# Lightning attention with an ELU layer on one core: a weight slice uncast on SyncE's queue, chunks 0 to 3 in pairs, decayed k made once, and a new order

## The chip, the cores and the metric

One Trainium2 chip, of which the program uses one core. The metric is the device time of one execution in microseconds (us). Three executions of the kernel before took 216.35, 214.18 and 216.23 us, the median is 216.23 us. Lower is better.

## What is computed

Decayed causal attention over `(B, H, S, D) = (4, 8, 768, 64)`, then a two-layer network without a gate:

```python
intra = (q_b @ k_b.T) * Dmask          # Dmask[i, j] = lam**(i - j) for i >= j, else 0
inter = (q_b * lam**(pos + 1)) @ kv_state
attn  = intra @ v_b + inter            # block by block along the sequence
kv_state = lam**block * kv_state + (k_b * lam**(block - 1 - pos)).T @ v_b
x = attn as [3072 tokens, 512]
h = x @ w_in                           # w_in [512, 2048]
g = where(h > 0, h, exp(min(h, 0)) - 1)
out = g @ w_out                        # w_out [2048, 512], out in float32
```

All inputs are float32 in memory. The kernels work in float16 with float32 sums.

## The kernel before

The 3072 tokens are cut into 24 chunks of 128: chunk `g` is sequence block `g // 4` of batch `g % 4`. So chunks 0 to 3 have no state behind them, and chunk `g` needs the state that chunk `g - 4` left. The last four leave none.

**Attention of one chunk.** `T`: q and k are transposed, for chunks 0 to 7 on TensorE (`att_T_pe`, L274: q comes out of PSUM times `qs`, the powers of lambda along the row, on VectorE; k by a copy on ScalarE), for chunks 8 to 23 by DMA transposes on SyncE's queue (`att_T_dma`, L264). `S`: eight matmuls give the scores of the eight heads in two PSUM banks (`att_S`, L294). `E`: VectorE multiplies each half with `mask`, which holds the causal triangle and the other half of the decay (`att_E`, L313). `P`: 8 matmuls with v, and from chunk 4 on 8 more with the state (`att_P`, L327). `X`: the result is written to `xt` in float16, on ScalarE for chunks 0 to 7, on VectorE with `qs` after that. `U`: `kd` (k times its decay, made on GpSimd, `att_kd`, L169) times v gives the state's growth (`att_U`, L388); `M`: GpSimd multiplies the old state with `upp` (`att_M`, L368), and VectorE adds the growth.

**The network.** `mm1` (L467) fills one PSUM tile `psH` of 128 x 512 (two such buffers): for chunks 0 to 3 one chunk by 4 columns of 128 of `w_in`, 16 matmuls of 128 x 128; from chunk 4 on two chunks by 2 columns, 8 matmuls of 128 x 256 (`GSIZE`). ScalarE takes `Exp` and then `Relu` of the tile, VectorE joins them to `g` (`flush`, L452), and this frees the buffer. `mm2` (L490) is 4 matmuls of 128 x 512; four such units make one chunk's output, which ScalarE copies and SyncE's queue stores. The very last columns of chunk 23 come in `mm2_rest` (L506). Each weight is held whole in float16 in 8 slices (`i0` to `i7` of w_in, `o0` to `o7` of w_out, each 256 KB in float16).

**What sets the order.** Every engine works in the order in which the code emits. The opening is written out by hand in `OPEN` (L53); after it a rule (L589 to L628) puts the attention of two chunks ahead of the mm1 units that need them, and up to two mm2 units behind each mm1. GpSimd has an order of its own, `POOL_ORDER` (L47): it issues all casting loads (float32 in memory, float16 on chip), and does `kd` and `M` between them. A load is issued only when the load 8 places ahead of it has landed. Only `lam` and the q of chunk 0 (`raw_q0`, float32, cast on VectorE, L122) come over SyncE's queue. PSUM has the two `psH` buffers and six other banks, given out by `BANKS` and by a rule (L255). Matmuls on zeros keep TensorE busy at the start: 10, then `w2` and `w6` in `OPEN`.

Of the kernel before, what the change touches and what calls it, by code (L numbers as in the profile page):

```python
# [15 lines left out]
def kernel(  # L16
# [26 lines left out]
    GSIZE = {**{g: 1 for g in range(4)}, **{g: 2 for g in range(4, NG, 2)}}  # L43
# [3 lines left out]
    POOL_ORDER = (  # L47
        "k0 k1 iota q1 k2 v1 i0 v0 q2 i1 v2 i2 o0 i3 d0 q3 o1 i4 k3 i5 o2 o3 v3 d1 m4 d2 d3 i7 "
        "o4 o5 i6 o7 k4 o6 q4 m5 k6 v4 q6 k10 q10 d5 d4 d6 m6 v6 k8 q8 v8 d7 m7 v10"
    )  # L50
    RAW = "q0"
    FIRST = "q0:0 c0 c1 c2"
    OPEN = (  # L53
# [7 lines left out]
    )  # L61
    LAGU = 7
    AT = {"L": -18, "W": -13, "T": -9, "S": -8, "B": -4}
    BANKS = (
        "S0=M0,M1 S1=C,D S2=D,M1 S3=D,B P0=M1 P1=B P2=B P3=D U0=M0 U1=D U2=A U3=M1 T0=M1,C "
        "T1=D,A T2=A,D T3=D T4=M0 T5=A T6=M1 T7=D M2=C M3=M0"
# [14 lines left out]
    def zero_matmuls(n):  # L81
# [4 lines left out]
    zero_matmuls(10)  # L86
# [4 lines left out]


# [3 lines left out]
    st = [  # L96
        [cpool.tile([128, NHP, 128], FP16, name=f"st{b}_{i}") for i in range(2)]
        for b in range(B)
    ]
    qg, kg, vg = {}, {}, {}  # L100

    def emit_load(w, g0):
        n = size_of[g0]
        c, b = divmod(g0, B)
        x = {"q": q, "k": k, "v": v}[w]
        src = x[b : b + n, :, c * L : (c + 1) * L].rearrange("b h p d -> p (b h) d")
        t = asb.tile([128, n, H, 64], FP16, tag=f"{w}n{n}", name=f"{w}n{g0}", bufs=4)
# [12 lines left out]
    nc.scalar.preload_act_table_set("natural_log_exp_and_others")  # L120

    def cast_raw(g, w, eng):  # L122
        n = f"{w}{g}"
        t = asb.tile([128, 1, H, 64], FP16, tag=f"{w}n1", name=f"{w}n{g}", bufs=4)
        (qg if w == "q" else kg)[g] = t
        if eng == 0:
            nc.vector.tensor_copy(t[:, 0], raw[n][:])
        else:
            nc.scalar.copy(t[:, 0], raw[n][:])

    def of(tiles, g):
        g0, i = group_of[g]
        return tiles[g0][:, i]
# [18 lines left out]

    def emit_wo(i):
# [9 lines left out]
    def emit_iota():  # L163
        nc.gpsimd.iota(iota_c[:], pattern=[[0, 1]], base=0, channel_multiplier=1)
        nc.gpsimd.iota(iota_r[:], pattern=[[1, 128]], base=0, channel_multiplier=0)

    kds, qkT, Pt, psS, xg = {}, {}, {}, {}, {}

    def att_kd(g):  # L169
        if g // B == NCB - 1:  # L170
            return
        kd = asb.tile([128, H, 64], FP16, tag="kd", name=f"kd{g}", bufs=8)
        kds[g] = kd
        nc.gpsimd.tensor_tensor(  # L174
            out=kd[:], in0=of(kg, g),
            in1=ks[:].unsqueeze(2).broadcast_to([128, H, 64]), op=ALU.mult,
        )


    pool_list = POOL_ORDER.split()  # L180

    def emit_pool():
        w = pool_list.pop(0)
        if w == "iota":
            emit_iota()
        elif w[0] in "qkv":
            emit_load(w[0], int(w[1:]))
        else:
            {"i": emit_wi, "o": emit_wo, "d": att_kd, "m": lambda g: att_M(g)}[w[0]](int(w[1:]))

    def emit_pool_run():
        while pool_list and pool_list[0][0] != "m":
            emit_pool()

    assert "iota" in POOL_ORDER.split("d0")[0]
    while pool_list and pool_list[0][0] not in "dm":
        emit_pool()

    def zero_st1(b):
        nc.vector.memset(st[b][1][:], 0.0)  # L200


    loglam = cpool.tile([128, H], FP32, name="loglam")
    nc.scalar.activation(loglam[:], lam_b[:], AF.Ln)
    pos = cpool.tile([128, 3], FP32, name="pos")
# [4 lines left out]

    dn = cpool.tile([128, H], FP32, name="dn")
    mask = cpool.tile([128, H, 128], FP32, name="mask")
    qs = cpool.tile([128, NHP, 128], FP32, name="qs")
    ks = cpool.tile([128, H], FP32, name="ks")
    upp = cpool.tile([128, NHP], FP32, name="upp")
    nc.vector.tensor_copy(row[:], iota_r[:])
    nc.vector.tensor_copy(pos[:, 0:1], iota_c[:])
    nc.vector.tensor_scalar_mul(pos[:, 1:2], iota_c[:], -1.0)
    nc.scalar.activation(dn[:], loglam[:], AF.Exp, scale=pos[:, 1:2])
    nc.vector.tensor_scalar(  # L220
        out=ident16[:], in0=row[:], scalar1=pos[:, 0:1], scalar2=None, op0=ALU.is_equal
    )
    nc.vector.tensor_scalar(
        out=causT[:], in0=row[:], scalar1=pos[:, 0:1], scalar2=None, op0=ALU.is_ge
    )
    for hh in range(2):
        r = slice(hh * 64, (hh + 1) * 64)
        nc.vector.tensor_copy(loglam_p[r, :], loglam[r, hh::2])
    nc.vector.tensor_scalar_add(pos[:, 2:3], pos[:, 1:2], float(L))

    def emit_qs():
        for hp in range(NHP):
            nc.scalar.activation(
                qs[:, hp, :], row[:], AF.Exp, scale=loglam_p[:, hp : hp + 1]
            )

    def emit_mask():
        nc.vector.tensor_tensor(
            out=mask[:],
            in0=causT[:].unsqueeze(1).broadcast_to([128, H, 128]),  # L240
            in1=dn[:].unsqueeze(2).broadcast_to([128, H, 128]),
            op=ALU.mult,
        )

    def emit_ks():
        nc.scalar.activation(ks[:], loglam[:], AF.Exp, scale=pos[:, 2:3])
        nc.scalar.activation(upp[:], loglam_p[:], AF.Exp, scale=float(L))

# [13 lines left out]


    def att_T_dma(g):  # L264
        ts = []
        for w, tiles in (("q", qg), ("k", kg)):
            t = asb.tile([128, NHP, 128], FP16, tag=f"{w}T", name=f"{w}T{g}", bufs=6)
            nc.sync.dma_start_transpose(
                out=t[:], in_=of(tiles, g).rearrange("p h d -> p (h d)")
            )  # L270
            ts.append(t)
        qkT[g] = ts

    def att_T_pe(g):  # L274
        n = len(TAGS[f"T{g}"].split())
        pts = [
            bank(f"T{g}", i, [128, 2 // n, NHP, 128], FP16, f"psT{g}_{i}")
            for i in range(n)
        ]
        pts = [pts[0][:, 0], pts[n - 1][:, 2 // n - 1]]  # L280
        for src, pt in zip((of(qg, g), of(kg, g)), pts):
            for hp in range(NHP):
                nc.tensor.transpose(  # L283
                    pt[:, hp, :], in_=src[:, 2 * hp : 2 * hp + 2, :], identity=ident16[:]
                )
        qt, kt = [
            asb.tile([128, NHP, 128], FP16, tag=f"{w}T", name=f"{w}T{g}", bufs=6)
            for w in "qk"
        ]
        nc.vector.tensor_tensor(out=qt[:], in0=pts[0], in1=qs[:], op=ALU.mult)  # L290
        nc.scalar.copy(out=kt[:], in_=pts[1])  # L291
        qkT[g] = (qt, kt)

    def att_S(g):  # L294
        qt, kt = qkT[g]
# [11 lines left out]
    late, X_done, Y_done, E_done = [], set(), set(), set()  # L307

    def until(done, g):
        while g not in done:  # L310
            late.pop(0)()

    def att_E(g):  # L313
        pts = psS.pop(g)

        def half(hh):
# [5 lines left out]
            if hh == 1:  # L322
                E_done.add(g)
# [3 lines left out]
    def att_P(g):  # L327
        cb, b = divmod(g, B)
        until(E_done, g)
        if cb > 0:  # L330
            until(Y_done, g - B)
# [295 lines left out]
    for t in prog:  # L627
        run(t)  # L628
# [34 lines left out]
```

## Time and profile before

| | us |
|---|---|
| three executions | 216.35, 214.18, 216.23 |
| span of the profiled execution | 213.2 |
| TensorE busy in it | 202.7 |
| VectorE, ScalarE, GpSimd busy | 130.1, 129.0, 96.2 |
| DMA queue of GpSimd's loads | 13.50 MB |
| DMA queue of SyncE | 10.76 MB |

The span runs from the first to the last instruction that the profiler sees; the time of an execution also holds what lies around it. The time of the profiled execution itself is not listed apart from the three; against their median the span is 3.0 us short. Busy times of TensorE overlap from one matmul to the next, so its pace is read from the starts of consecutive groups.

### The profile page before, as it was taken

The page shows a single profiled execution, that of the slowest core. Times are in us where ns is not written, and L with a number is a line of the kernel's source. Part 1 is how long each engine was busy: PE and PEld are TensorE (multiplying, and loading weights), DVE is VectorE, ACT ScalarE, POOL GpSimd, SP SyncE. Part 2 cuts the span into 40 slices and gives each one's busy share as a digit, 9 for nine tenths or more (in the row PEclk, how much of TensorE's full clock was granted, in tenths as well). Part 3 has the DMA queues.
Part 4 walks back from the last instruction along what each step waited for, and adds up shares of the span by engine and source line. Part 5 has one row for each costly group of instructions (what it writes and reads, how often), then busy time and mean ns, then how long its engine had stood idle before and what let it go on. Part 6 is the DMA issues. An engine that isn't in the chain of part 4 may idle for free.

```text
span 213.2 us, 5156 instructions
## 1 busy us (share of the span) xinstructions
PE 202.7 (95%) x2066; PEld 138.1 (65%) x2066; DVE 130.1 (61%) x224; ACT 129.0 (61%) x245; POOL 96.2 (45%) x115
## 2 busy tenths in 40 slices
PE   7667999999999999999999999999999999999994
PEld 2355676767686776766766766766766666666652
DVE  3936453777846888677667667667667547533321
ACT  4545654884867756676476476476476576477640
POOL 7996991999972908667166259300000000000000
PEclk9999999999999999999999999999999999999999
DMA  8999999999996999999939919999124110110112
GB/s 90 141 175 193 192 148 173 147 165 147 153 165 145 111 197 107 144 122 116 129 106 125 167 59 103 144 180 161 52 65 83 52 49 0 54 51 16 36 49 98
DMA packets 101976, 24.59 MB, mean 115 GB/s; under 512 B 92608, under 2 KB 99008, under 8 KB 101952
## 3 DMA queue, kind: packets, MB, share of 16 engines
q0 software_dynamic: 79760, 13.50, 83.1%
q1 hardware_dynamic: 22192, 10.76, 24.6%
q8 instruction: 16, 0.26, 0.5%
q14 instruction: 8, 0.07, 0.1%
HBM read 27.27 MB, written 6.29 MB: 157 GB/s over the span
## 4 chain that ended last, share of the span: by engine, by line
PE 82%; POOL 8%; DMA 7%; issue 1%; ACT 1%; DVE 0%; POOLq 0%; ACTq 0%
PE psM L499 36%; PE psH L478 35%; DMA wi<-in_moe_w_in_dram 4%; DMA wo<-in_moe_w_out_dram 3%; PE psO L338 3%; PE psS L302 3%; PE psO L344 2%; POOL kd L174 1%; POOL wi L148 1%; POOL kn L109 1%; POOL vn L109 1%; PE psU L406 1%; PE psT L283 1%; POOL qn L109 1%; POOL wo L155 1%
## 5 line engine op out<-in xcount | busy, mean ns | idle before, releaser
L478 PE MATMUL psH<-xt,wi 128*128 128x256 f16 (+1 forms) x896 | 99.3, 258 | 2.0 <-DMA wi<-in_moe_w_in_dram 1.1
L457 DVE SCALAR_TENSOR_TENSOR g<-e,psH 128x512 f16<-128x512 f32 x96 | 65.8, 686 | 56.7 <-ACT psH L485 56.0
L484 ACT ACTIVATE e<-psH 128x512 f32<-128x512 f32 x96 | 57.3, 597 | 65.0 <-PE psH L478 62.8
L499 PE MATMUL psM<-wo,g 128*128 128x512 f16 (+1 forms) x384 | 95.6, 377 | 0.7 <-DMA wo<-in_moe_w_out_dram 0.7
L478 PEld LDWEIGHTS <-wi 128*128 128x128 f16 x896 | 76.9, 98 | 27.4 <-DMA wi<-in_moe_w_in_dram 1.8
L485 ACT ACTIVATE psH<-psH 128x512 f32<-128x512 f32 x96 | 57.0, 593 | 0.0
L499 PEld LDWEIGHTS <-g 128*128 128x128 f16 x384 | 35.9, 98 | 29.3 <-issue 1.3
L318 DVE TENSOR_TENSOR pp<-psS,mask 128x512 f16<-128x512 f32 x48 | 30.8, 684 | 4.4 <-PE psS L302 4.4
L174 POOL TENSOR_TENSOR kd<-kn,ks 128x512 f16<-128x512 f16 x20 | 20.7, 1040 | 21.3 <-DMA kn<-in_k_dram 20.4
L378 POOL TENSOR_TENSOR stt<-st,upp 64x256 f32<-64x256 f16 x32 | 19.5, 608 | 14.7 <-DVE st L418 8.9
L109 POOL DMA_DIRECT2D vn<-in_v_dram x14 | 15.5, 1108 | 1.7 <-DMA wi<-in_moe_w_in_dram 1.7
L109 POOL DMA_DIRECT2D kn<-in_k_dram x14 | 15.5, 1105 | 0.8 <-POOLq L647 0.8
L525 ACT COPY osb<-psM 128x512 f32<-128x512 f32 x23 | 13.5, 590 | 3.2 <-PE psM L499 3.2
L109 POOL DMA_DIRECT2D qn<-in_q_dram x13 | 14.8, 1138 | 0.0
L418 DVE TENSOR_TENSOR st<-stt,psU 64x256 f16<-64x256 f32 x32 | 13.3, 416 | 1.2 <-PE psU L406 0.5
L361 DVE TENSOR_TENSOR xt<-psO,qs 128x512 f16<-128x512 f32 x16 | 11.0, 688 | 3.5 <-PE psO L344 3.5
L338 PE MATMUL psO<-pp,vn 128*64 128x128 f16 x192 | 12.0, 222 | 1.2 <-DMA vn<-in_v_dram 1.0
L338 PEld LDWEIGHTS <-vn 128*64 128x64 f16 x192 | 9.7, 110 | 4.6 <-issue 2.9
L344 PE MATMUL psO<-qT,st 128*64 128x128 f16 x160 | 10.0, 219 | 0.0
L344 PEld LDWEIGHTS <-st 128*64 128x64 f16 x160 | 8.9, 110 | 0.0
L302 PE MATMUL psS<-qT,kT 64*128 64x128 f16 x192 | 7.9, 218 | 0.3 <-ACT kT L291 0.3
L359 ACT CAST xt<-psO 128x512 f16<-128x512 f32 x8 | 4.4, 588 | 6.4 <-PE psO L338 4.3
(44 smaller groups left out, 72.3 us busy)
## 6 DMA issues: line engine op xcount, KB each, us to landing
out_dram<-osb SPq DMA_DIRECT2D x23, 256.0 KB, 2.2
kn<-in_k_dram POOLq DMA_DIRECT2D x10, 256.0 KB, 7.8
qn<-in_q_dram POOLq DMA_DIRECT2D x10, 256.0 KB, 6.8
vn<-in_v_dram POOLq DMA_DIRECT2D x10, 256.0 KB, 7.6
wi<-in_moe_w_in_dram POOLq DMA_DIRECT2D x8, 256.0 KB, 6.9
wo<-in_moe_w_out_dram POOLq DMA_DIRECT2D x8, 256.0 KB, 7.7
kn<-in_k_dram POOLq DMA_DIRECT2D x4, 128.0 KB, 4.2
vn<-in_v_dram POOLq DMA_DIRECT2D x4, 128.0 KB, 5.5
```

The source lines that it names most:

```text
L109: nc.gpsimd.dma_start(out=t[:].rearrange("p b h d -> p (b h) d"), in_=src)
L174: nc.gpsimd.tensor_tensor(out=kd[:], in0=of(kg, g), in1=ks[:].unsqueeze(2).broadcast_to([128, H, 64]), op=ALU.mult,)
L302: nc.tensor.matmul(psS[g][hh][:, hp, :], lhsT=kt[r, hp, :], rhs=qt[r, hp, :], start=True, stop=True,)
L318: nc.vector.tensor_tensor(out=P[:], in0=pts[hh][:], in1=mask[:, hh::2, :], op=ALU.mult)
L338: nc.tensor.matmul(po[r, hp, :], lhsT=vt[:, 2 * hp + hh, :], rhs=Pt[(g, hh)][:, hp, :], start=True, stop=(cb == 0), skip_group_check=True,)
L344: nc.tensor.matmul(po[r, hp, :], lhsT=st[b][cb % 2][:, hp, r], rhs=qt[:, hp, :], start=False, stop=True, skip_group_check=True,)
L378: nc.gpsimd.tensor_tensor(out=tmp[r], in0=old[r, :, r], in1=upp[r].unsqueeze(2).broadcast_to([64, NHP, 64]), op=ALU.mult,)
L457: nc.vector.scalar_tensor_tensor(out=g[:].rearrange("p f c t -> p (f c t)"), in0=e[:], scalar=-1.0, in1=r[:], op0=ALU.add, op1=ALU.min,)
L478: nc.tensor.matmul(pH[:, f * n * 128 : (f + 1) * n * 128], lhsT=wi16[i][:, kk, w * 128 : (w + 1) * 128], rhs=xg[g0][:, kk, :], start=(kk = ...
L484: nc.scalar.activation(e[:], pH[:], AF.Exp)
L485: nc.scalar.activation(pH[:], pH[:], AF.Relu)
L499: nc.tensor.matmul(psM[g][:, cols], lhsT=gts[(g, j * FB + f)], rhs=wo16[i][:, w, cols], start=first and f == 0, stop=end and f == FB - 1, ...
```

## The change

- **Opening loads.** `raw_q0` goes; slice `i1` of w_in comes in float32 over SyncE's queue (512 KB), and ScalarE casts it (`cast_wi`). q of chunk 0 becomes a casting load of GpSimd. GpSimd's order becomes `k0 q0 k1 i3 (iota) q1 k3 q3 v0 v1 q2 k2 i2 v2 i0 v3 k4 q4 o2 o3 v4 (kd5) i4 o1 o0 i7 k6 i6 q6 o7 i5 o6 o4 o5 (kd7 kd6) k8 ...`. Before, it was `k0 k1 (iota) q1 k2 v1 i0 v0 q2 i1 v2 i2 o0 i3 (kd0) q3 o1 i4 k3 i5 o2 o3 v3 (kd1, M4, kd2, kd3) i7 o4 o5 i6 o7 k4 o6 q4 ...`.
- **Pairs.** `GSIZE` is 2 everywhere: mm1 has 96 units of 8 matmuls of 128 x 256 (before 16 units of 16 matmuls of 128 x 128, and 80 of 8).
- **Decay of k.** `kd` is made for all 24 chunks, 11 of them on VectorE (0 to 3 and 4, 10, 14, 15, 20, 22, 23), and it is `kd`, not k, that is transposed; so `E` multiplies with the plain triangle `causT`, and `mask` and `dn` go.
- **State.** VectorE adds the growth to the state in float32, and GpSimd multiplies the sum with `upp` into the state (before: GpSimd first, VectorE last); for the first block VectorE does the product alone.
- **Order.** One list `ORDER` holds every step of every engine. The zero matmuls are the first 10 alone. Banks are in `BANKS` for every step. The last units are `R` (`mm2_rest`), then mm2 of chunks 22 and 19.

The diff, cut to its core:

```diff
-    GSIZE = {**{g: 1 for g in range(4)}, **{g: 2 for g in range(4, NG, 2)}}
+    GSIZE = {g: 2 for g in range(0, NG, 2)}
-    RAW = "q0"
-    FIRST = "q0:0 c0 c1 c2"
+    RAW = "i1S"
+    ORDER = (
+        "z:0:1:v z:1:1:v L:k0 z:1:0:a L:q0 L:k1 log logp i:3 upp c:1:a iota col L:q1 row ks caus qs:0 qs:2 "
+        "ident qs:1 d:0:v qs:3 L:k3 t:q0 z:0:0:v t:k0 e:q0:v L:q3 e:k0:a d:1:v s:0 L:v0 t:k1 E:0:0 e:k1:a "
+        "E:0:1 L:v1 t:q1 e:q1:v L:q2 d:3:v s:1 L:k2 E:1:0 t:q3 t:k3 e:q3:v e:k3:a i:2 u:0 p:0 E:1:1 s:3 x:0:a "
+        "L:v2 E:3:0 p:1 z:2:0:a x:1:a y:0 i:0 t:q2 z:2:1:a 1:0:3 E:3:1 L:v3 d:2:v 1:0:1 h:0:3 e:q2:v L:k4 "
+        "t:k2 e:k2:a g:0:3 L:q4 h:0:1 s:2 1:0:2 E:2:0 o:2 E:2:1 h:0:2 o:3 g:0:1 p:2 u:2 x:2:v L:v4 u:3 p:3 "
+        "u:1 g:0:2 1:0:0 x:3:a z:3:1:v 1:2:0 h:0:0 d:5:p d:4:v y:1 t:k4 i:4 h:2:0 t:k5 g:0:0 t:q4 o:1 t:q5 "
+        "e:q4:v 1:2:1 e:k4:a o:0 g:2:0 s:4 h:2:1 e:q5:v i:7 1:2:2 E:4:0 L:k6 2:1:1 e:k5:a E:4:1 h:2:2 g:2:1 "
+        "s:5 i:6 2:0:1 E:5:1 L:q6 y:3 1:2:3 g:2:2 o:7 u:4 h:2:3 p:4 E:5:0 u:5 i:5 1:2:4 y:5 x:4:a g:2:3 p:5 "
...
+        "g:22:4 2:20:0 h:20:6 2:22:2 g:20:6 2:23:2 2:20:3 2:21:3 R 2:22:0 2:19:2"
+    )
+    def cast_wi(i, eng):
+        if eng == "a":
+            nc.scalar.copy(out=wi16[i][:], in_=raw[f"i{i}"][:])
...
+    def att_kd(g, eng="p"):
+        kd = asb.tile([128, H, 64], FP16, tag="kd", name=f"kd{g}", bufs=8)
+        kds[g] = kd
+        {"v": nc.vector, "p": nc.gpsimd}[eng].tensor_tensor(
+            out=kd[:], in0=of("k", g),
+            in1=ks[:].unsqueeze(2).broadcast_to([128, H, 64]), op=ALU.mult,
+        )
...
+    def att_E(g, hh):
+        P = asb.tile([128, NHP, 128], FP16, tag="pp", name=f"pp{g}_{hh}", bufs=6)
+        nc.vector.tensor_tensor(
+            out=P[:], in0=psS[g][hh][:],
+            in1=causT[:].unsqueeze(1).broadcast_to([128, NHP, 128]), op=ALU.mult,
+        )
...
+    def att_Y(g, hh):
...
+            nc.vector.tensor_tensor(
+                out=tmp[r], in0=stp[b][cb % 2][r, :, r], in1=src, op=ALU.add
+            )
```

In `ORDER`, `L`, `i` and `o` are loads; `d` is `kd`; `t` and `e` are a TensorE transpose and its way out of PSUM; `D` a DMA transpose; `s`, `E`, `p`, `x`, `u` are the steps named above; `y` and `m` the state on VectorE and on GpSimd; `1:g:j` a unit of mm1, `h` its two ScalarE steps, `g:` VectorE's join; `2:g:j` a unit of mm2. A last letter `a`, `v` or `p` says ScalarE, VectorE or GpSimd. So `1:2:4` is the unit of chunks 2 and 3 on slice `i4`.

More of the change, by code (lines that the diff above doesn't have):

```diff
@@ L161 @@
     iota_r = cpool.tile([128, 128], I32, name="iota_r")
[L163 to L200, printed above, removed]
     loglam = cpool.tile([128, H], FP32, name="loglam")
-    nc.scalar.activation(loglam[:], lam_b[:], AF.Ln)
-    pos = cpool.tile([128, 3], FP32, name="pos")
+    col = cpool.tile([128, 2], FP32, name="col")
     row = cpool.tile([128, 128], FP32, name="row")
@@ L219 @@
[L219 to L242, printed above, removed]
-        )
-    def emit_ks():
-        nc.scalar.activation(ks[:], loglam[:], AF.Exp, scale=pos[:, 2:3])
-        nc.scalar.activation(upp[:], loglam_p[:], AF.Exp, scale=float(L))
+    def emit_iota():
+        nc.gpsimd.iota(iota_c[:], pattern=[[0, 1]], base=-L, channel_multiplier=1)
+        nc.gpsimd.iota(iota_r[:], pattern=[[1, 128]], base=-L, channel_multiplier=0)
@@ L397, in att_U @@
+    def att_U(g):
+        if g < B:
+            pu = bank(f"U{g}", 0, [128, NHP, 64], FP32, f"psU{g}")
+        elif g % 2 == 0:
+            psUU[g] = bank(f"U{g}", 0, [128, 2, NHP, 64], FP32, f"psU{g}")
+            pu = psUU[g][:, 0]
+        else:
+            pu = psUU[g - 1][:, 1]
+        vt = of("v", g)
+        for hp in range(NHP):
+            for hh in range(2):
+                r = slice(hh * 64, (hh + 1) * 64)
                 nc.tensor.matmul(
-                    full[:, hp, :].rearrange("p (h e) -> p h e", h=2),
@@ L445 @@
-    gts, psM, stores, pending = {}, {}, [], []
+                    pu[r, hp, :], lhsT=kds[g][:, 2 * hp + hh, :], rhs=vt[:, 2 * hp + hh, :],
+                    start=True, stop=True, skip_group_check=True,
+                )
+        psU[g] = pu
+    gts, psM, psH, stores, pending = {}, {}, {}, [], {}
     def emit_stores(keep=0):
@@ L627 @@
-    for t in prog:
-        run(t)
-    mm2_rest()
-    while late:
-        late.pop(0)()
+    CONST = {
+        "iota": emit_iota, "col": const_col, "row": const_row, "log": const_log,
+        "qn": const_qn, "ks": const_ks, "ident": const_ident, "caus": const_caus,
+        "logp": const_logp, "upp": const_upp,
+    }
+    def run(t):
+        if t in CONST:
+            CONST[t]()
+            return
+        w, *a = t.split(":")
+        n = [int(x) if x.isdigit() else x for x in a]
+        if w in "Late" and a[0][0] in "qkv":
+            x, g = a[0][0], int(a[0][1:])
+            {"L": emit_load, "a": scaled, "t": att_T_pe, "e": att_T_out}[w](x, g, *a[1:])
+        elif w == "D":
+            att_T_dma(a[0][0], int(a[0][1:]))
+        elif w == "y":
+            att_Y(n[0], 0)
+            att_Y(n[0], 1)
+        else:
+            {"qs": const_qs, "z": zero_st, "w": zero_matmuls, "i": emit_wi, "o": emit_wo,
+             "c": cast_wi, "d": att_kd, "s": att_S, "E": att_E, "p": att_P, "x": att_X, "u": att_U,
+             "m": att_M, "1": mm1, "h": elu_in, "R": mm2_rest, "g": elu_out, "2": mm2}[w](*n)
@@ L632 @@
+    for t in ORDER.split():
+        run(t)
     emit_stores()
```

404 lines of the change are left out of this document (138 added, 266 removed), and 50 rows, old and new, of tables (BANKS, OPEN, ORDER).

## Prediction

> **What bounds the kernel now.** I read the page first (shares, slices, chain), then windows of 10 us, then TensorE's timeline, and at last the DMA view on windows so narrow that they hold one load, which gives its landing.
>
> ```profile
> span 213.2 us, 5156 instructions
> PE 202.7 (95%) x2066; PEld 138.1 (65%) x2066; DVE 130.1 (61%) x224; ACT 129.0 (61%) x245; POOL 96.2 (45%) x115
> PE   7667999999999999999999999999999999999994
> PE 82%; POOL 8%; DMA 7%; issue 1%; ACT 1%; DVE 0%; POOLq 0%; ACTq 0%
> ```
>
> TensorE is full from the fifth slice on; the chain leaves it only in the opening (POOL and DMA, 15%).
>
> ```profile
> core 0: us, PE busy (x) PEld busy (x) DVE busy (x) ACT busy (x) POOL busy (x), PEclk, DMA share, GB/s
> 0.00:10.00 10.00, 6.76 (x46) 2.99 (x47) 6.53 (x19) 5.33 (x14) 8.88 (x16) 1.00 1.31 112
> 10.00:20.00 10.00, 7.24 (x105) 5.22 (x103) 5.57 (x10) 5.21 (x10) 8.97 (x12) 1.00 1.72 181
> 20.00:30.00 10.00, 9.18 (x108) 6.56 (x108) 5.46 (x9) 6.21 (x12) 9.13 (x12) 1.00 1.44 175
> 30.00:40.00 10.00, 9.65 (x119) 6.82 (x118) 4.20 (x8) 5.38 (x11) 5.20 (x7) 1.00 1.58 172
> 60.00:200.00 140.00, 139.78 (x1385) 96.07 (x1383) 89.74 (x149) 88.75 (x166) 44.47 (x51) 1.00 0.89 103
> ```
>
> TensorE idles 7.2 us in the first 40 us and 0.2 us after that. So only the opening can be shortened; after it the change can save matmul time or make new waits, no more. In the opening GpSimd is at 0.9 (it issues loads) while VectorE is at 0.55: the loads bind there.
>
> ```profile
> 38.63 1.07 PE L478 MATMUL psH<-xt,wi 128*128 128x128 f16 x16
> 39.53 0.39 PE L397 MATMUL psU<-vn,kd 128*128 128x128 f16 x4
> 93.17 1.04 PE L478 MATMUL psH<-xt,wi 128*128 128x256 f16 x8
> 94.04 1.03 PE L499 MATMUL psM<-wo,g 128*128 128x512 f16 x4
> 94.90 1.04 PE L478 MATMUL psH<-xt,wi 128*128 128x256 f16 x8
> 209.03 1.06 PE L511 MATMUL psMrest<-wo,g 128*128 128x128 f16 x16
> ```
>
> From start to start: a paired mm1 unit 0.87, an mm2 unit 0.86, a single mm1 unit 0.90 us. The last matmul ends at 210.1; the span's other 3.1 us are the way out.
>
> ```profile
> 88.45 0.69 DVE L457 SCALAR_TENSOR_TENSOR g<-e,psH 128x512 f16<-128x512 f32 x1 [1.05 <-ACT psH L485]
> 89.09 0.69 DVE L361 TENSOR_TENSOR xt<-psO,qs 128x512 f16<-128x512 f32 x1
> 89.70 0.69 DVE L457 SCALAR_TENSOR_TENSOR g<-e,psH 128x512 f16<-128x512 f32 x1
> ```
>
> VectorE's steps of 128x512 follow each other every 0.61 to 0.64 us.
>
> **Check of the paces.** The attention of two chunks with state takes 2.06 us (the chain's score groups start 15.92 us apart, less 8 x 0.87 and 8 x 0.86); without U 1.7. After 39.9 us the windows by line count 688 matmuls of mm1 (80 paired, 3 single units) and 348 of mm2 (83 whole units and 2.6 us of cut ones): 69.6 + 2.7 + 71.6 + 2.6, last part 0.9, 8 x 2.06 and 2 x 1.7 attention, 2.3 transposes and single U, 0.2 idle: 169.8. The trace has 170.2, so I add 0.4%.
>
> **Part 1, pairs.** 16 single units become 16 paired ones: 16 x (0.90 - 0.87) = 0.5 us less on the path. ScalarE and VectorE still have 96 tiles. It is inside the sum below.
>
> **Part 2, the opening.** GpSimd issues a 128 KB load every 0.88 us, a weight slice every 0.75. Landings before: q1 issued 3.48, landed 4.4 later; v0 6.84 and 5.2; i1 8.58 and 5.8; in a backlog a 128 KB load lands 0.87 us after the one ahead, a weight slice 1.35, a 256 KB pair of chunks 1.8. `raw_i1` (512 KB) has no row: `raw_q` (256 KB) landed at 4.5, 3.3 after its issue, and a slice of 512 KB at its source costs 1.35 in a backlog; 4.5 and half of 1.35 give 5.2, and I take 5.3, nearest to the slice's row (bounds 4.5 as `raw_q`, and 7.8 with its 3.3 doubled, of which the waits for v3 and k4 below would take up all but some 1 us). Placing the new queue at these paces: q0 6.3, k1 7.2, i3 8.6, q1 9.7, k3 10.8, q3 11.8, v0 12.8, v1 13.7, q2 14.6, k2 15.6, i2 17.1, v2 18.0, i0 19.4, v3 20.3, k4 22.1, q4 23.9, o2 25.2, o3 26.5, v4 28.3, i4 29.6, o0 32.3, i7 33.6, o7 39.8, o6 42.5, o5 45.1. Weights thus come 5 to 8 us later than before (o7 36.9, o6 40.1).
>
> Now the chain, with 0.4 for 4 transposes or 8 score matmuls to their end, 1.09 for ScalarE's two steps, 0.58 for its copy. GpSimd's iota slips behind four loads: 4.8 (before 3.22). ScalarE casts `i1` (two rows of 0.59, 5.3 to 6.4), then `ks`, then `qs` to 8.0. kd0 on VectorE 6.7 to 7.3 (no row; nearest `qT` 0.68 and half of `mask` 0.60; I take 0.61 in a row of steps; bounds 0.6 and GpSimd's own 1.04). qT0 8.0, S0 8.65 to 9.05 (before 8.50). From here VectorE is the chain: kd1, E0, qT1, kd3, E1, qT3, E1: 13.5. P1 14.2, its copy on ScalarE 15.0, first mm1 unit at 15.05 (before 13.37, but for half the columns). Next E3, kd2 (k2 15.6), qT2 17.05; S2 17.9; g 17.9 frees `psH`: third unit 18.3. P2, U2, U3 (v3 20.3), P3, U1 21.05; fourth unit 21.05, fifth 21.95. kd4 waits for k4 (22.1), then y1, g, qT4, g, qT5, E4, E4, g, E5, y3, g to 29.9, every 0.61 to 0.8: unit six 24.3, seven 25.6, mm2 on o2 and o3 26.55 and 27.7, unit eight 28.5, unit nine (`1:2:4`, i4 29.6) at 30.3. TensorE idles about 2.3 us of 15.05 to 30.3.
>
> **Part 3, what is left then.** 88 paired units 76.6; 90 mm2 units 77.7, the cut ones 2.6, last part 0.9; P5 0.5; transposes 0.9; 7 x 2.06 and 2 x 1.7 attention 17.8: 177.0, with 0.4% 177.7. 30.3 + 177.7 = 208.0.
>
> **Part 4, new waits after that.** Before, one of 0.2 us. VectorE gets 11 kd of 0.61 and 3 copies, loses `mask` (1.2) and a cast (0.7): 130 to about 136 us, cover for it is TensorE's 200. But around the sixth to ninth chunk (nominal 54 to 66 us) about 15 VectorE steps stand in one row, 10 us, and mm1's buffers need the g among them: 0.5. `1:0:4` waits 0.3 behind g. DMA transposes of the last k wait for kd23 on VectorE, with 2.7 us to land and 2.9 in hand, and v16 is issued behind the state's step `m` on GpSimd with 1.4 in hand: 0.5 for both. In SyncE's queue the stores stand behind such transposes, and their buffers (four) hold 16 us of work. Sum 1.3; bounds 0 (all covered, as before) and 4 (each of these 1 us). 208.0 + 1.3 = 209.3.
>
> **Part 5, the way out.** Before: copy 0.27 and a 64 KB store of 1.6 us behind the last matmul. Now the last is a whole chunk: copy 0.59, store 256 KB 2.2 us. 3.1 + 0.3 + 0.6 = 4.0.
>
> **Sum.** 209.3 + 4.0 = 213.3 us against the execution's 213.2. Executions stand 1.0 to 3.2 above this span, their median 3.0: 213.3 + 3.0 = 216.3 us. No change: the opening is filled less well until 15 us and better after it.
>
> **Rivals.**
> (a) TensorE goes back to half pace. The ten zeros took 4.00 us, 0.40 each, where later ones start 0.2 apart: it starts at half pace and needs about 4 us of work to leave it. Place: 5 to 15 us, where it now works some 3 of 10 us and `w2` and `w6` (8 zeros) are gone. It decides if such sparse work counts as idle. 4 us of the first mm1 work at half pace cost 2.0, three early groups 0.2 each: 2.6, so 218.9. Against it: a gap of 1.31 us at 6.6 did no harm before, and my longest is 1.6. The Trainium skill, "TensorE: Matmul & The Clock Gate", Part 1, speaks against the change here: TensorE falls back to half clock after one idle window of about 3.4 us. By that rule gaps of 1.6 us do nothing and the sum stands; if a window of sparse work counts as idle, it is this rival and its 218.9. No row of this trace tells which.
> (b) VectorE's row is slower: 30 steps from kd0 to the ninth unit. If each takes 0.69 plus a hop of 0.02 and not 0.61, 30 x 0.1 = 3.0 us: 219.3. It decides from 0.66 on, where the idle left to the loads (k4, v3) is used up. For it: most VectorE steps before stand alone with 0.69; kd with GpSimd's 1.04 would do the same. Against: the rows above.
> (c) Faster: mm1 never waits for a buffer between 15 and 30 us, because the paired units need half the weights and the loads land as early as before's first ones (4.4 after issue). The 2.3 us idle and 0.8 of part 4 go: 213.2. It decides if k4 and v3 land 1.5 us sooner than placed. For it: GpSimd's queue of small loads has less backlog. Against: VectorE's row stands anyway.
> (d) The weights are late: mm2 on o6 and o7 comes at about 45 with o6 at 42.5. At 5% less pace the reserve is gone, at 10% it costs 2 us: 218.3. Before, the gap-ridden mean pace (6.2 MB by 41.8) gives 43.5 for o6.
>
> **How the numbers follow.** No change 0.45; (a) 0.12, (b) 0.13, (d) 0.10, (c) 0.20. 1% (2.2 us) is about what a measurement of this kernel can tell from no change. Faster 0.2, within 1% 0.47, slower 0.33 (of (d)'s 0.10 some 0.02 stay within). Range: from (c), 213.2, to (b) with half a microsecond of part 4, 219.8; the likeliest alone 215.0 to 218.2.
>
> **What would show it.** First mm1 unit at 15.05, `1:2:4` at 30.3, last matmul at 209.3, VectorE over 0.8 busy from 8 to 34 us, o6 landed by 43. Zeros gone and single starts of 0.11 us for 128 columns after 10 us would show (a); ends of g on VectorE past 31 for `g:2:2` (b); psM waiting for wo (d). I am wrong if the stretch after 45 us has idle TensorE of over 2 us.

## Result, and the profile after

| | us |
|---|---|
| after: median of 4 executions | 222.09 (220.88 to 223.35) |
| before: median of 4 executions | 215.65 (214.18 to 216.35) |
| ratio after / before, 95% interval | 1.031 (1.024 to 1.038) |
| span of the profiled execution after (before 213.2) | 221.6 |

Slower by 3.1%. I had said 216.3, no change, with 213.2 to 219.8 as the range. Three of the kernels below had one execution of four more than 1.5% above their fastest, which the times given for them leave out.

The profiled execution is the slowest of the four, 223.35 us, at a mean granted clock of 0.968; the fastest, 220.88 us, had 0.991, a sign that it lost less to half pace than the trace read here.

The page of the changed kernel (the span, then TensorE's busy row and its granted clock in 40 slices of 5.5 us):

```profile
span 221.6 us, 4887 instructions
...
PE   7488999999959999599999999999999999999992
...
PEclk9859999999979999799999999999999999999999
```

Before, TensorE's row was 9 from the fifth slice on. Now two slices show a 5, at 61 to 66 us and at 89 to 94 us, and the clock dips with each, and a third time at 10 to 16 us. TensorE's two longest waits behind 40 us (in all, times, longest):

```profile
PE psS L328 <- DMA kT<-kd: 2.6, 1, 2.6
PE psU L419 <- DMA vn<-in_v_dram: 2.4, 1, 2.4
```

One wait is for the transposed k of chunk 9, the other for v of chunk 12. What follows each is seen in TensorE's timeline (start, duration, the idle time before in brackets):

```profile
58.35 1.05 PE L451 MATMUL psH<-xt,wi 128*128 128x256 f16 x8
59.23 1.89 PE L475 MATMUL psM<-wo,g 128*128 128x512 f16 x8
63.68 0.63 PE L328 MATMUL psS<-qT,kT 64*128 64x128 f16 x16 [2.55 <-DMA kT<-kd]
64.24 1.89 PE L451 MATMUL psH<-xt,wi 128*128 128x256 f16 x8
65.92 1.85 PE L475 MATMUL psM<-wo,g 128*128 128x512 f16 x4
67.61 1.04 PE L451 MATMUL psH<-xt,wi 128*128 128x256 f16 x8
...
88.42 1.04 PE L451 MATMUL psH<-xt,wi 128*128 128x256 f16 x8
91.81 0.42 PE L419 MATMUL psU<-vn,kd 128*64 128x64 f16 x8 [2.35 <-DMA vn<-in_v_dram]
```

Behind the first wait a unit takes 1.68 us from start to start (64.24, 65.92, 67.61) where it took 0.87: TensorE runs at half pace for two units and loses 1.64 us more. Behind the second the steps of P follow each other by 0.107 us per pair of matmuls and not 0.055; with U on either side that costs some 1.6 us (half of the 3.13 from 91.81 to 94.94). The windows (us, busy times, then PEclk as the third number from the right) say the same:

```profile
64.00:66.00 2.00, 2.00 (x21) 1.40 (x16) 1.67 (x3) 0.00 (x0) 1.09 (x2) 0.54 1.47 228
66.00:68.00 2.00, 2.00 (x9) 0.89 (x8) 1.70 (x5) 1.09 (x2) 0.00 (x0) 0.61 1.46 228
68.00:70.00 2.00, 2.00 (x14) 1.11 (x13) 0.92 (x4) 1.09 (x2) 0.00 (x0) 1.00 1.65 156
92.00:94.00 2.00, 2.00 (x46) 2.00 (x44) 0.87 (x2) 0.00 (x0) 0.00 (x0) 0.50 1.64 228
```

The account: the last matmul ends at 217.65 (forecast 209.3), 8.35 late. Opening 0.5, waits 2.55 and 2.35, half pace 1.64 and 1.6: 8.6. The 0.3 by which this is too much is what was left of the 1.3 us that I had added for new waits: four short waits for VectorE (0.16 to 0.24) took 0.8 of it, and the work itself was 0.2 longer than forecast. The way out, 3.95, is as forecast (4.0).

Why the data is late, in the DMA view of 50 to 66 us, first of the kernel before, then of the changed one (number of issues, KB each, median us from issue to landing):

```profile
vn<-in_v_dram POOLq DMA_DIRECT2D x2, 256.0 KB, 6.5
qT<-qn SPq DMA_TRANSPOSE x3, 2.5
kT<-kn SPq DMA_TRANSPOSE x2, 2.6
```

```profile
kn<-in_k_dram POOLq DMA_DIRECT2D x3, 256.0 KB, 13.7
out_dram<-osb SPq DMA_DIRECT2D x3, 256.0 KB, 6.6
vn<-in_v_dram POOLq DMA_DIRECT2D x2, 256.0 KB, 17.3
kT<-kd SPq DMA_TRANSPOSE x4, 7.7
qT<-qn SPq DMA_TRANSPOSE x4, 8.1
```

Before, the transposes came as the loads ran out (the last one was issued at 55.70, the first transpose at 58.05); now they share the DMA engines with a backlog (k14, k16, v14 ahead of k12, q12, v10) and land 7.7 to 8.1 us after their issue, not 2.5. kT of chunk 9 was issued at 54.95 and landed at 63.7. v12 was issued at 82.98 and took 8.8 us to land. It stands late in GpSimd's order, and GpSimd had stood 6.4 us at k12 ahead of it:

```profile
71.53 2.04 POOL L275 TENSOR_TENSOR kd<-kn,ks 128x512 f16<-128x512 f16 x2 [6.38 <-DMA kn<-in_k_dram]
...
82.98 2.36 POOL L159 DMA_DIRECT2D vn<-in_v_dram  x2
```

Nor could v12 have gone before 80 us: v14, loaded early, had taken the fourth buffer of v, and the next one comes free with P of chunk 9, at 80 us.

### The profile page after: what moved, and what is told of

Read it like the earlier page. It is cut to its first block, busy times and chain, and to the rows that moved or that the text cites. A ratio compares the mean times of both kernels' runs of the same rounds, so it can differ in the third digit from the quotient of the medians.

```text
span 221.6 us, 4887 instructions
## 1 busy us (share of the span) xinstructions
PE 205.5 (93%) x1946; PEld 138.7 (63%) x1946; DVE 136.4 (62%) x236; ACT 128.5 (58%) x242; POOL 90.7 (41%) x108
## 4 chain that ended last, share of the span: by engine, by line
PE 74%; DMA 13%; DVE 7%; issue 2%; POOL 2%; ACT 1%; POOLq 0%; SPq 0%; ACTq 0%
PE psM L475 32%; PE psH L451 32%; DMA vn<-in_v_dram 4%; DMA kT<-kd 4%; PE psS L328 3%; DMA qT<-qn 3%; DVE g L436 2%; DMA qn<-in_q_dram 2%; PE psO L349 2%; PE psO L355 2%; PE psTq L304 1%; DVE stt L402 1%; DVE pp L335 1%; PE psU L419 1%; POOL kn L159 1%
## 5 line engine op out<-in xcount | busy, mean ns | idle before, releaser
L451 PE MATMUL psH<-xt,wi 128*128 128x256 f16 x768 | 97.9, 275 | 0.6 <-DVE g L436 0.6
L475 PE MATMUL psM<-wo,g 128*128 128x512 f16 (+1 forms) x384 | 93.2, 379 | 0.0
L451 PEld LDWEIGHTS <-wi 128*128 128x128 f16 x768 | 74.0, 99 | 23.8 <-issue 1.4
L386 POOL TENSOR_TENSOR stp<-stt,upp 64x256 f16<-64x256 f32 x32 | 20.5, 640 | 60.6 <-DVE stt L402 59.2
L335 DVE TENSOR_TENSOR pp<-psS,causT 128x512 f16<-128x512 f32 x48 | 31.7, 683 | 6.4 <-PE psS L328 6.2
L275 POOL TENSOR_TENSOR kd<-kn,ks 128x512 f16<-128x512 f16 x13 | 13.7, 1070 | 9.4 <-DMA kn<-in_k_dram 7.1
L402 DVE TENSOR_TENSOR stt<-stp,psU 64x256 f32<-64x256 f16 x32 | 13.3, 415 | 1.3 <-PE psU L419 0.7
L355 PE MATMUL psO<-qT,stp 128*64 128x128 f16 x160 | 11.7, 233 | 0.0
L328 PEld LDWEIGHTS <-kT 64*128 64x128 f16 x192 | 5.8, 97 | 8.9 <-issue 3.3
L355 PEld LDWEIGHTS <-stp 128*64 128x64 f16 x160 | 9.8, 120 | 0.0
```

Source lines behind the costliest of these rows:

```text
L328: nc.tensor.matmul(psS[g][hh][:, hp, :], lhsT=kt[r, hp, :], rhs=qt[r, hp, :], start=True, stop=True,)
L335: nc.vector.tensor_tensor(out=P[:], in0=psS[g][hh][:], in1=causT[:].unsqueeze(1).broadcast_to([128, NHP, 128]), op=ALU.mult,)
L355: nc.tensor.matmul(po[r, hp, :], lhsT=stp[b][cb % 2][:, hp, r], rhs=qt[:, hp, :], start=False, stop=True, skip_group_check=True,)
L386: nc.gpsimd.tensor_tensor(out=new[r, :, r], in0=stt.pop((g, hh))[r], in1=upp[r].unsqueeze(2).broadcast_to([64, NHP, 64]), op=ALU.mult,)
L402: nc.vector.tensor_tensor(out=tmp[r], in0=stp[b][cb % 2][r, :, r], in1=src, op=ALU.add)
L451: nc.tensor.matmul(pH[:, f * n * 128 : (f + 1) * n * 128], lhsT=wi16[i][:, kk, w * 128 : (w + 1) * 128], rhs=xg[g0][:, kk, :], start=(kk = ...
```

## Experiments

Diffs of the order are given in its own words: `L:k14` is the load, `D:k9` the transpose. "The stretch" is from S of chunks 6/7 to S of chunks 14/15 in the profiled execution: 50.2 us in the changed kernel; without its two waits and their half pace (8.1) it would be 42.1.

**1. Near loads first.**

```diff
- L:k14 ... L:k16 L:v14 L:k12 L:q12 L:v10 ... L:k18 d:16:p ... L:v12 L:v22
+ L:k12 L:q12 L:v10 ... L:k14 ... L:k16 d:16:p L:k18 ... L:v12 L:v14 L:v22
```

> Only the order of GpSimd's loads changes (and with it the step d:16:p): k12, q12 and v10 go ahead of k14, k16 and v14, v12 ahead of v14 and v22, k18 and q22 later; so k14 to v14 neither stand in front of loads that are needed sooner nor hold the buffers. Theory 1 (loads made too far ahead run beside the DMA transposes and hold the four buffers of v, which makes kT of chunk 9 and v12 late): fewer loads are under way at 52 to 64 us, kT9 lands 5 to 6 us after its issue and not 8.7, TensorE's wait at 61.1 us falls from 2.55 to under 0.5, GpSimd's wait of 6.4 us for k12 shrinks, v12 is issued before 78 us, the wait at 89.5 us (2.35) goes, and with both the stretches at half clock (1.64 and 1.6 us): 222.1 - 8.1 = 214 us, between 213.5 and 217. Theory 2 (transposes behind each other and behind stores on SyncE's queue are slow by themselves, whatever the loads do): kT9 still takes 8 to 9 us, the first wait and its half clock stay, only the second goes: 218 us. Theory 3 (new waits grow elsewhere as soon as these go, since the new order has no reserve): 219 us and more.

236.28 us, ratio 1.096 (1.090 to 1.101). Theories 1 and 2 missed; new waits grew elsewhere, as theory 3 had it. The first wait grew to 3.0: kT of chunk 9 took 8.6 us beside the near loads alone, so it is not the far loads as such. And GpSimd reached v12 only at 92 us, behind kd16, kd18 and kd19, whose k16 and k18 I had put late: a wait of 8.7, and one of 3.9 for transposes that stood in SyncE's queue behind that of k19, which was issued at 90.9. In a queue that is worked in order, one late load held up everything behind it.

**2. v12 early.**

```diff
- ... L:v10 ... L:v12 L:v22        v: bufs=4
+ ... L:v10 L:v12 ... L:v22        v: bufs=5
```

> v12 is issued straight behind v10, and v gets a fifth buffer so that this load need not wait for P of chunk 9 to give back the buffer that v14 holds. All else stays. If the second wait (2.35 us at 89.5) comes from v12 alone, and the half clock after it (1.6 us) from that wait, then both go, 3.9 us: 218.2 us (217.5 to 219); the first wait at 61.1 us stays or grows by up to 0.5. Rival: U of chunk 12 has another wait just behind v12's (a transpose or kd12), and the time falls by under 1.5 us: 220.6 and more.

220.92 us, 1.028 (1.024 to 1.033). The second wait and its half clock are gone, and the stretch is 47.0. But the first wait rose to 3.55, with one load more beside the transposes. The mechanism held. The time fell by 1.2 us in the median where I had said 3.9, and the intervals of the two ratios overlap.

**3. Zeros in the waits.**

```diff
+        for _ in range(FILL_S.get(g, 0)):     # {9: 11}; before U of chunk 12: 10
+            nc.tensor.matmul(psS[g][0] as 128x512, zero16[:, 0:128], zero16, start=True, stop=True)
```

> The waits stay; TensorE does matmuls on zeros in them: 11 of 128x512 in front of S of chunk 9 (into its own PSUM bank, which S then writes anew) and 10 in front of U of chunk 12. If half the price of each wait is the clock that falls behind it, the clock stays at 1.0 at 64 to 68 and 92 to 96 us, and 1.64 + 1.6 us go: 218.9 us (218.3 to 220). If the half clock has another cause than the idle time (sparse or small matmuls, the work of another engine), it stays: 222.1 us, or up to 1 us more where the zeros outlast the waits.

224.02 us, 1.038 (1.031 to 1.044). The clock did what I said, the time did not. Windows of this run:

```profile
64.00:66.00 2.00, 2.00 (x23) 1.33 (x18) 1.72 (x3) 0.67 (x2) 0.98 (x1) 1.00 1.48 229
66.00:68.00 2.00, 2.00 (x15) 1.30 (x14) 1.97 (x6) 1.35 (x3) 0.00 (x0) 1.00 1.46 229
...
88.00:90.00 2.00, 2.00 (x9) 1.14 (x8) 2.00 (x4) 0.64 (x2) 1.78 (x4) 0.50 1.94 157
```

Kept busy, TensorE has its full clock at 64 to 68: the half clock comes from the idle time. But TensorE came 1.6 us sooner to the next chunks, and their transposes were not there: 0.34 and 0.78 us at 71, and 2.15 at 86.9 for a q, with half clock behind it.

**4. Zeros in the opening.**

```diff
+ w:6 before t:q0, w:4 before s:0, w:2 before t:q1, w:3 before s:1   (w: zero matmuls of 128x512)
```

> Zeros in the gaps of the opening: 6 of 128x512 ahead of the first transpose, 4 ahead of S of chunk 0, 2 ahead of the transposes of q1, 3 ahead of S of chunk 1. If the half clock from 10 to 16 us comes from idle time, it goes and the granted clock is 1.0 until the first wait at 61 us. What it is worth: my rival (a) priced it at 2.6 us; the trace of the changed kernel says 0.5 at most (the first mm1 unit came at 15.64 where I had 15.05), since loads and VectorE's row bind there and TensorE's work is short. So 221.6 to 222.1 by the trace, 219.5 by rival (a). If the zeros do not hold the clock, 222.1 and the same 0.50 from 10 to 16 us.

221.80 us, 1.030 (1.027 to 1.034). Clock 1.00 from 6 to 60 us, first mm1 unit at 14.78 (15.64), `1:2:4` at 30.45 (30.80): half clock in the opening was worth some 0.4 us here. It was given back: at 61 us TensorE still waited 1.82, and at 86 us 2.30 for a q transpose in place of the wait for v12, with half clock behind both.

**5. Loads held.**

```diff
- L:k14 ... L:k16 L:v14 L:k12 L:q12 L:v10 m:9
+ m:9 L:k12 L:q12 L:v10 L:k14 L:k16 L:v14          (d:16:p to d:18:p)
```

> In GpSimd's order the six loads k12, q12, v10, k14, k16, v14 (so the near ones first) stand behind the state's step of chunk 9 at 59 us, and d:16:p goes to d:18:p; nothing else moves. So no load is issued between 46 and 59 us, while the transposes of chunks 8 and 9 are made. Theory 1b (after the miss of the first run, where only the near loads stood there and kT of chunk 9 still took 8.6 us: a transpose is late beside any backlog of loads, near or far): kT9 lands 2.5 to 5 us after its issue, TensorE's wait at 61 us and its half clock go (4.2 us), and the time is 218 us if the wait for v12 stays, 214 if it goes too; the loads of chunk 12 come no later than now (71 us), as their backlog is shorter. Theory 2 (transposes and stores on SyncE's queue hold each other): kT9 takes 8 us as before, the wait stays, 222 us or more.

227.39 us, 1.060 (1.054 to 1.065). In a window that holds the issue of kT9 alone:

```profile
kT<-kd SPq DMA_TRANSPOSE x1, 4.3
```

4.3 us instead of 8.7, and no wait at 61 us. So loads beside it do make a transpose late. But the held loads then stood beside the transposes of chunks 10 and 11 (8.2 and 8.7 us): 2.52 and 1.31 at 72, and 3.45 for v12. The time is above 222, where theory 2 had put it, but from these new waits and not from its mechanism.

**6. Stores on ScalarE's queue.**

```diff
-            nc.sync.dma_start(out=dst, in_=o)
+            nc.scalar.dma_start(out=dst, in_=o)
```

> The stores of the output are issued on ScalarE's queue and not on SyncE's; all else stays. Theory 2 (transposes are late because stores stand among them in SyncE's queue): the three stores between 51 and 62 us no longer part the transposes, each of which follows the one before by 1.4 us, so kT9 is issued 0.9 us sooner and lands in under 6 us: wait 1 under 0.5 us, time 218 us or less. Theory 1b (the engines are shared with the loads): kT9 lands only as much sooner as it is issued sooner, the wait stays over 1.5 us: 221 to 222.5 us.

223.65 us, 1.042 (1.038 to 1.045). Transposes became slower still; the same DMA view:

```profile
out_dram<-osb ACTq DMA_DIRECT2D x3, 256.0 KB, 10.2
...
kT<-kd SPq DMA_TRANSPOSE x4, 11.2
qT<-qn SPq DMA_TRANSPOSE x4, 10.0
```

The wait for kT9 was 5.9 us. Theory 2 falls: taking the stores out of SyncE's queue did not help its transposes, and with a third queue at work they took longer still. The time is above theory 1b's 222.5 as well.

**7. q first.**

```diff
- D:k8 D:q9 D:q8 D:k9
+ D:q9 D:q8 D:k8 D:k9
```

> In SyncE's queue the transposes of q9 and q8, whose load has landed at 47.9 us, go ahead of that of k8, which waits for kd8 until 50.0 us; nothing else moves. In the changed kernel all four stand behind that wait for kd8, so kT9 is issued at 54.95 although kd9 is ready at 51. Theory 4 (the order within SyncE's queue makes half of the first wait): kT9 is issued at 52.3, lands 2 us or more sooner, TensorE's wait at 61 us is under 1 us and the clock does not fall: 2.55 + 1.6 less, 218 us, unless the second wait grows by what the first gives (then 220 to 221, as where zeros filled the opening or the waits: each time TensorE came sooner, it waited for a q transpose at 85 us instead). Theory 1b: what is issued sooner lands at the pace of the shared engines, the wait falls by 1 us at most: 221 us.

222.75 us, 1.037 (1.032 to 1.041). The wait at 61 us is gone: kT9 was issued at 53.5. So theory 4 held at this place, but not in the time (218, or 220 to 221): TensorE then waited 2.48 and 0.77 at 72 us, for the transposes of chunks 10 and 11, and 1.42 for v12. And `1:2:4` came at 32.24 in this execution, 1.4 later than in the changed kernel, though the opening is the same: half pace lasted to 19 us, not to 16.

**8. Loads and transposes in order of use.**

```diff
- L: k14 k16 v14 k12 q12 v10 k18 q14 q16 q22 v12 v22 q18 ...   D: k8 q9 q8 k9 k11 q10 ... k19 q15 ...
+ L: k12 q12 v10 v12 q14 k14 q16 k16 v14 k18 v16 q18 ...       D: q9 q8 k8 k9 q10 q11 k11 k10 q13 q12 k13 k12 ...
```

> TensorE's, ScalarE's and VectorE's orders stay; the loads of GpSimd stand in the order in which their chunks are used (k12 q12 v10 v12 q14 k14 q16 k16 v14 ...), kd13 and kd12 ahead of kd16, kd18, kd19, the transposes of SyncE in the order of use with q ahead of k (that of k19 no longer among those of chunk 12 and 14), v has six buffers, the transposed tiles eight. If the late transposes and v12 are all that the new order costs (theory 1b with 4), no wait of over 1 us is left behind 40 us, the clock stays full from 20 us on, and the time is 222.1 - 8 = 214 us (213.5 to 216), as much as the kernel before. If the engines' total pace is what binds up to 95 us (theory 5: the new order uses chunks 8 to 13 sooner than the DMA engines can bring them, in whatever order), waits of 2 us or more stay at 61 or 85 us: 218 us and more.

221.75 us, 1.030 (1.027 to 1.034). Still 2.6 at 61 us (a store stood between the transposes of q9 and q8, and waited for its copy), and 2.3 for the state, as kd16 waited for k16 ahead of GpSimd's step M. I took this for theory 5, too hastily.

**9, 10. Attention later; and with order of use and zeros.**

```diff
- s:8..17 behind 40 40 47 47 59 59 74 74 83 83 units
+ s:8..17 behind 46 46 57 57 69 69 85 85 100 100 units
```

> Only the place of the attention of chunks 8 to 17 in the order of TensorE (and of the VectorE, ScalarE and GpSimd steps that hang on it) changes: its S steps stand behind 46, 57, 69, 85 and 100 units of the network, about where the kernel before has them (46.9, 58.7, 72.7, 87.9, 103.9 units, counted in its trace), and not behind 40, 47, 59, 74 and 83. The units between are the same, drawn from the chunks that are ready; v has six buffers, the transposed tiles eight; loads and transposes keep their order. Theory 5 (the DMA engines are full up to 95 us and more, and the new order asks for the data of chunks 8 to 17 some 6 to 13 units, 5 to 11 us, sooner than the kernel before, sooner than they can come): no wait of over 1 us behind 40 us, the clock stays full there: 214 us (213.5 to 216.5). Rival: the order of loads and transposes themselves is at fault (far loads first, q behind k): a wait of 2 us or more stays, 219 us or more.

> The same places of the attention, and with them the loads and transposes in the order in which their chunks are used (as in the run with the mended order, but kd16 behind the state's steps that are needed sooner), 12 buffers for kd, and the zeros in the gaps of the opening. Theory 5: as the run beside it, less 0.4 to 1 us for the opening: 213 us (212.5 to 215). If the new order of loads makes new waits, 217 us or more, and the run beside it is the better one.

238.70 us (1.109) and 239.86 us (1.113). No wait for a DMA was left behind 40 us in either, but mm1 units now stood in rows and TensorE waited 10.7 and 11.0 us for g. Inconclusive.

**11. Stores held.**

```diff
-        emit_stores(1)
+        if mm1_count[0] > 50: emit_stores(max(1, len(stores) - 2))
+        elif mm1_count[0] <= 18: emit_stores(1)
```

> All orders of the changed kernel stay; only the output stores between the 18th and the 50th mm1 unit (about 45 to 95 us) are held back and issued behind it, up to two or more to a unit, for which the output buffers go from 4 to 14. That takes some 8 stores of 256 KB out of the stretch in which the DMA engines are full, and nothing else. Theory 5 (sum of the DMA work): the waits of TensorE at 61 and 89 us shrink together by 3 us or more, 219 us or less. Rival (the sum does not matter, only what stands ahead of what in GpSimd's queue of loads): waits and time as they are, 221.5 to 223 us.

220.58 us, 1.024 (1.017 to 1.030). The second wait went: v12, issued at 82.4, landed 5.1 us later, not 8.8. The first stayed at 2.9. The two waits together fell by 2.0 us, where theory 5 asked for 3, and the rival for none.

**12, 13, 14. Twins with late and early attention.**

```diff
- s:8 s:10 s:12 s:14 s:16 behind 46 58 72 87 103 units   (12; 14 adds the zeros of run 4)
+ s:8 s:10 s:12 s:14 s:16 behind 42 47 59 74 83 units    (13)
```

> From 46 us on the order of all engines is written anew, by one rule for this run and for its twin: mm1 and mm2 units in turn, each step as soon as its inputs are there, loads and transposes in the order in which their chunks are used, the buffers as in the run with later attention (kd 12). S of chunks 8, 10, 12, 14, 16 stands behind 46, 58, 72, 87 and 103 units, as in the kernel before. The run with later attention had no wait for a DMA left but 10.7 us of waits for g, as several mm1 units stood in a row ahead of it; here they alternate. Theory 5 (demand ahead of supply): no wait for a DMA of over 0.5 us behind 40 us and a full clock; work of 46 to 208 us, 214.5 us (213 to 216.5). If a wait for a transpose or a load of 2 us or more stays even so, theory 5 is wrong.

> The twin: the same rule, the same order of loads and transposes and the same buffers, but S of chunks 8, 10, 12, 14, 16 behind 42, 47, 59, 74 and 83 units, as the changed kernel has them. Theory 5: waits for transposes or loads of 3 us or more together between 55 and 95 us, and half clock behind each that is over 2 us: 3 to 7 us above its twin, 217.5 to 221.5 us. Rival (the changed kernel's order of loads is at fault, not the spacing): no such waits, the same time as its twin within 1 us.

> The run with the late spacing and, in the opening, the zeros of the run that filled the opening's gaps (6, 4, 2 and 3). Full clock from 5 us on; 0.3 to 1 us under the late spacing alone, 214 us (212.5 to 216). If both kernels before lie above it, it is the version to carry on with.

227.73, 229.51 and 228.21 us (1.058, 1.066, 1.063): far above the forecasts, with many waits of 0.2 to 2.0 us for VectorE that my order made, so they are no better kernels. But the early twin speaks on theory 5. Its S steps:

```profile
63.91 0.62 PE L327 MATMUL psS<-qT,kT 64*128 64x128 f16 x16
71.10 0.62 PE L327 MATMUL psS<-qT,kT 64*128 64x128 f16 x16
85.45 0.62 PE L327 MATMUL psS<-qT,kT 64*128 64x128 f16 x16
```

They start when those of the changed kernel do (63.68, 72.05, 85.25), and no bracket stands behind them: the data was there. The changed kernel asks for chunk 9 sooner, at 61.1, where kT9 of the twin has not landed (61.7); but in run 18, below, these steps start at 61.4, 68.4 and 81.9 with one wait of 0.44 among them. So the DMA engines can bring the data in time for these places, and theory 5 as I put it falls: most of the waits come from the order. That the sum has no part in them is not shown, as run 18 also holds the stores back, which by itself took 2.0 us of the waits in run 11.

**15, 16. Waits mended; with zeros and way out.**

```diff
+ D: q9 q8 k8 k9 q10 q11 k11 k10 q13 q12 k13 k12    L: k12 q12 v10 v12 k14 k16 v14
+ d:10:v before E:6:1, stores held as in 11, v: bufs=6, qT and kT: bufs=8
+ (16) zeros as in 4; R (the last part of chunk 23) at the very end
```

> TensorE's and ScalarE's orders are those of the changed kernel. Mended is only what makes chunks 8 to 13 late: in SyncE's queue the transposes of q go ahead of those of k (q9 q8 k8 k9, q10 q11 k11 k10, q13 q12 k13 k12), the output stores are held back between the 18th and the 50th mm1 unit, kd10 moves to a slack place of VectorE, GpSimd loads k12, q12, v10, v12 ahead of k14, k16, v14, and v and the transposed tiles have 6 and 8 buffers. Account of the miss (the two waits of 2.55 and 2.35 us, each with 1.6 us of half clock behind it, are the whole difference to my forecast but the 0.5 of the opening): no wait over 0.5 us behind 40 us, full clock from 20 us on, last matmul at 209 to 211 us, and the time is my old sum, 216 us (214.5 to 217). Rival: there is a further cost in the new order that the waits hide, and the time stays above 218.

> The run beside it with the zeros in the gaps of the opening (6, 4, 2, 3) and with the last part of chunk 23 as the very last work, as in the kernel before: 0.4 to 1 us less in the opening, 0.9 us less behind the last matmul: 214.5 us (213 to 216), about the kernel before or a little under it.

220.76 us, 1.026 (1.023 to 1.030), and 220.84 us, 1.025 (1.023 to 1.027). In run 15 no wait for a DMA was left behind 40 us, and the clock was full from 20 us on; but P waited 2.8 us for the state: kd16 ahead of M again, 11.2 us at k16. And `1:2:4` came at 32.43, 1.6 later than in the changed kernel. In run 16 one wait for a transpose was left, 1.32.

**17, 18. M mended too.**

```diff
- ... d:12:p d:16:p m:6 ... m:8 d:18:p       D: q10 q11 k11 k10
+ ... d:12:p m:6 ... m:8 d:16:p d:18:p       D: k10 q10 q11 k11
```

> The run with the mended waits had four waits of 2.8 us together for the state (P of chunks 8 to 12 behind GpSimd's step M), because I had put kd16, which waits 11.2 us for k16, ahead of M. Here kd16 stands behind M of chunk 8, and the transpose of k10 ahead of those of q10 and q11; nothing else differs from that run. From S of chunks 6/7 to S of chunks 14/15 the changed kernel takes 50.2 us, that run 46.0 with 2.8 us of waits. Account of the miss: 43.2 us there without waits, and 220.8 - 2.8 = 218.0 us (217 to 219). Rival (some other cost takes the place of these waits too): the stretch stays at 45 us or more, 220 us.

> The same mending with the zeros in the opening and with the last part of chunk 23 at the end. In the profiled executions S of chunk 4 starts at 25.3 us where zeros keep the clock up, and at 25.4 to 27.3 in the others. The run beside it less 1 us for the opening and 0.9 for the way out: 216.2 us (215 to 217), what I had forecast for the changed kernel; no clock below 1.0. Rival: opening and way out are hidden by something later, 218 us as beside it.

Run 17: 218.38 us, 1.016 (1.012 to 1.020). The stretch is 44.3, with these waits left in it (1.5 at 88 us), and no half clock in it:

```profile
PE psO L354 <- POOL stp L385: 1.5, 2, 1.1
```

Run 18: 218.63 us, 1.017 (1.013 to 1.021); its wait for the state was 1.74 and 0.44, and the clock fell behind it, which ate what the opening (`1:2:4` at 30.80, not 31.77) and the way out gave. No version here beats the kernel before.

## Why the prediction was wrong

- **Part 1, pairs, Part 2, opening:** right. Loads landed within 0.9 us of my list up to 50 us, mostly earlier (k4 21.2 for 22.1, o6 41.8 for 42.5); the first mm1 unit came at 15.64 (15.05), `1:2:4` at 30.80 (30.3). In other runs with this opening `1:2:4` came as late as 32.43 (run 15); see rival (a).
- **Part 3, what is left:** nearly right, 177.7 in the forecast. The changed kernel takes 186.85 from `1:2:4` to the last matmul; less 5.7 of waits and 3.24 of half pace that is 177.9. Run 17, from `1:2:4` at 31.77 to the last matmul at 212.77, takes 181.0; less its 2.1 us of waits 178.9. The 1.0 between the two is in no wait that the profile lists.
- **Part 4, new waits: the step that failed.** I wrote 1.3 us, with 4 as the upper bound; they were 4.9 us, and 3.2 more of half pace: 8.1. I looked for late data at the last k and v16 only. For the last k the "2.7 us to land" were right: the last four transposes, with no load beside them, took 2.4. But the transposes of chunks 8 to 13 and the load of v12, which the new order asks for with loads under way, have no term at all: I put them at nothing without a reason, and kT of chunk 9 took 8.7. The bounds had no term for a slower clock behind a wait. The rows to use were there: before, the transposes issued at 76.77 and 98.51 us, beside two or three loads each, took this long:

```profile
qT<-qn SPq DMA_TRANSPOSE x1, 7.4
kT<-kn SPq DMA_TRANSPOSE x1, 7.0
```

- **Part 5, way out:** right, 3.95 (4.0).
- **The offset.** I added 3.0 for what lies around the span, from the median of executions other than the profiled one. In all those of the changed kernel, the time is 1.75 to 1.80 above the span of the same execution. With that the sum would have been 215.1 and the miss 7.0, not 5.8: the wrong offset hid 1.2 us of it, by luck.
- **Rival (a), half pace in the opening:** it happened, at 10 to 16 us with a longest gap of 1.42. In the changed kernel's profile it cost 0.4 us and not 2.6, as loads and VectorE bind there: `1:2:4` at 30.80, and at 30.45 in run 4, where zeros hold the clock. In run 15 the same opening, at half pace to 18 us, reached it at 32.43; by that comparison it can cost 2.0. **(b), (c), (d):** not seen; VectorE's row and the weights kept to the list.
- My closing test, "wrong if the stretch after 45 us has idle TensorE of over 2 us", is what came about.

Shown: each of the two waits can be taken away (runs 2, 5, 7, 11), the half clock comes from the wait (3), and with both gone and the first wait for the state mended the loss falls from 3.1% to 1.6% (17). Open: the other 1.6%, 3.5 us. In run 17 some 2 us are waits and 0.8 is the longer way out; the rest, 0.7, I would put to the opening, but run 18, which was to show that, gained nothing in the time. Why the gain is not the whole 8.1: against the changed kernel's profile, run 17's last matmul comes 4.9 us sooner. Its `1:2:4` comes 1.0 later, it waits 1.5 for the state, and some 0.8 of the difference is in no listed wait.

## What to carry to other kernels

Take the time of a DMA from rows with the same neighbours under way: a transpose of 2.4 us alone was 8 us beside a backlog of loads. Where an order runs loads far ahead, ask of each queue what stands in front of the next needed transfer, and whose buffer the early load holds. Price a wait of TensorE with the slower clock behind it, and do not count a gain ahead of such a place before the next data is known to be there: in runs 3, 4, 7 and 18 what was won came back as the next wait.

## Hardware behaviour not expected

- **The clock falls after less idle time than I had allowed.** It halved behind waits of 1.74 and 0.44 in a row (run 18), 1.82 (run 4), 2.35 and 2.55 us, for about 3.5 us; it did not behind 1.44 and 0.44 in a row (16), nor behind one of 1.85 and one of 2.00 for g in runs 12 and 14. Every wait of 2.15 or more behind 40 us had half clock behind it. The Trainium skill, "TensorE: Matmul & The Clock Gate", Part 1, gives an idle window of about 3.4 us; these rows are shorter, and they decide. It also says that the window runs freely, so that the point at which the clock changes varies; that agrees with 2.00 doing nothing where 1.82 did, and with the opening: half pace from 10.1 us in one profile and from the first transpose at 6.96 in run 17 (four transposes 0.61 us, not 0.40).
- **The clock row can miss it.** In run 17 PEclk says 1.00 from 6 to 16 us, while these transposes take 0.61. Durations are the safer reading.
- **A transpose took longer, the more was under way beside it:** 2.4 us with no load (the last four of the changed kernel), 4.3 with the loads held, 7.7 beside loads and stores of the same queue, 11.2 with the stores in a queue of their own.
